# Scaling k by powers of gamma: from one POOL instruction to POOL and ACT, two pairs of heads each

## The chip, the cores and the metric

The program runs on one core of a Trainium2 chip. The metric is the device time of one execution, in microseconds (us). Engines are named as in the profile: PE (matmul; PEld is its weight load), DVE (vector), ACT (scalar), POOL (GpSimd) and SP (which here issues every DMA).

## The reference, cut to what matters

Three layers follow each other, all in float32. The change lies in the first.

```
scores = (q @ k^T) / 8                        # 8 batches, 8 heads, 576 positions, 64 features
ret    = scores * Dmat                        # Dmat[i, j] = gamma_h ** (i - j) for j <= i, else 0
x      = (ret @ v), heads side by side        # 4608 tokens x 512
logits = x @ phi ; d = softmax over tokens ; c = softmax over slots
slot_out = relu((d^T x) @ w1[e]) @ w2[e]      # 8 experts, 4 slots each
y      = c @ slot_out
out    = (((y @ m1) * (y @ m2)) @ w3) @ wo
```

## The kernel before, in words

The attention is done chunk by chunk. A chunk is 64 positions, there are 9 of them, and 8 batches are taken two at a time, so there are 36 steps (`u` from 0 to 35). A step holds two batches and all eight heads, the heads as four pairs. Within a chunk the scores are computed directly. What earlier chunks contribute comes through a running state of 64x64 per head, the sum of k times v. In that sum k of chunk c is multiplied by gamma to the minus position (divided by 8), and the state is multiplied by gamma to the chunk's first position when it is read out. `scale_k(w)` (line 139) does the first of these in place on the k half of the tile `vk`: 128 partitions x 512 elements, which are 2 batches x 4 pairs of heads x 64 features. It multiplies by a table `ktab_sb` that holds one number for each partition, chunk and pair. The first two of its 37 calls, before the loop, go to DVE and the other 35 go to POOL.

The order on each engine is the order in which the program issues, and each engine's queue is worked off in that order. Nothing is moved by a planner. One turn of the loop at line 551 issues, in this order:

- `scale_k(u+2)` on POOL; it waits for the DMA of `vk`, issued three turns earlier by `load_vk`.
- The split of weights. The kernel also turns the float64 weights of the last layer into float32 pieces during the attention. One piece is handled in a turn: an `Abs` on ACT (line 359), then five instructions on DVE (lines 360 to 363 and 354), then an addition on POOL (line 380). For some pieces a copy on ACT (line 385) and a subtraction on POOL (line 390) come a turn later. `run(subs)`, `run_copies()` and `run(adds)` issue these last three, `next_conv` starts the next piece with its `Abs`.
- `emit_qk_pv`: the scores of chunk u+2 (line 159) and the product with v of chunk u (line 161) on PE.
- `emit_p(u+2)`: the scores times the table of powers, DVE, line 167.
- `emit_xt(u)`: the result times its powers, DVE, line 197.
- `emit_state(u+1)`: on PE the new state (line 179, which reads the scaled k of chunks u+1 and u) and the readout of the old one (line 184). Then four instructions on ACT (line 191), one for each pair, that scale the state into SBUF.
- `load_vk(u+5)` and `load_qk(u+6)` on SP, when the buffers are free (six and five of them).
- transposes of x on PE (line 212) with a copy on ACT (line 213), and every fourth turn the logits, the softmax and the slot sums.
- the remaining instructions of the piece of weights on DVE (lines 360 to 354).

So POOL's queue holds in each turn `scale_k`, at times a subtraction, and an addition that waits for DVE's line 354. The `scale_k` of the next turn runs directly behind that addition. ACT's queue holds the copy of the turn before, then the copy or `Abs` for the weights, then the four of line 191.

After the loop the experts run (33.5 MB of weights through the buffers that the attention frees), then the last layer, whose matmuls are at lines 852 to 855.

Of the kernel before, what the change touches and what calls it, by code (L numbers as in the profile page):

```python
# [14 lines left out]
ACTF = mybir.ActivationFunctionType  # L15
ALU = mybir.AluOpType
# [6 lines left out]
NCH = S // 64  # L23
# [7 lines left out]
def retention_softmoe_bilinear(  # L31
# [15 lines left out]
    nc = tc.nc  # L47
# [49 lines left out]
    ktab_sb = tabs_sb[:, 256:292].rearrange("p (c k) -> p c k", c=9)  # L97
# [17 lines left out]
    def four(t):  # L115
        return t.rearrange("p (x k i) -> p x k i", x=2, k=4)

    def qk_tiles(u):
        t = qkb[u % QBUF]
        return four(t[:, 0:512]), four(t[:, 512:1024])  # L120

    def vk_tiles(w):
        t = vkb[(w + 1) % NBUF]
        return four(t[:, 0:512]), four(t[:, 512:1024])
# [6 lines left out]
    def span(w):  # L131
        return slice(0 if w >= 0 else 64, 128 if w < NU - 1 else 64)
# [6 lines left out]
    def scale_k(w, eng=nc.gpsimd):  # L139
        s = span(w)  # L140
        K = vk_tiles(w)[1][s]
        eng.tensor_tensor(  # L142
            out=K, in0=K, in1=ktab_sb[s, w % NCH].unsqueeze(1).unsqueeze(3).to_broadcast([s.stop - s.start, 2, 4, 64]), op=ALU.mult,
        )

    def qk_view(u):
        return four(bank[u % 2])
# [5 lines left out]
    def emit_qk_pv(u, w):  # L153
        for x in range(2):
            for p in range(4):
                for h, a, b in halves:
                    if u is not None:
                        Q, K = qk_tiles(u)
                        nc.tensor.matmul(out=qk_view(u)[a, x, p], lhsT=K[a, x, p], rhs=Q[a, x, p], start=True, stop=True)  # L159
                    if w is not None:  # L160
# [11 lines left out]
    def emit_state(u):  # L172
        c = u % NCH
        for p in range(4):
            for x in range(2):
                for h, a, b in halves:
                    if c < NCH - 1:
                        V, K = vk_tiles(u - h)
                        nc.tensor.matmul(  # L179
                            out=sbank[a, x, p], lhsT=K[a, x, p], rhs=V[a, x, p],  # L180
                            start=(c == 0 and x == 0 and p == 0), stop=True, skip_group_check=True,
# [318 lines left out]
    with tc.manual_schedule():  # L500
# [28 lines left out]
        emit_p(0)  # L529
        load_qk(5)  # L530
        scale_k(-1, nc.vector)
        scale_k(0, nc.vector)
        scale_k(1)
        warm(256)
        emit_qk_pv(1, None)
# [115 lines left out]
        for k in range(4):  # L651
# [7 lines left out]
            out=sme, in0=sT.rearrange("p k (e j) -> p e k j", j=4),  # L659
            in1=rzs.rearrange("p x (e j) -> p e x j", j=4).to_broadcast([128, 8, 4, 4]), op=ALU.mult,  # L660
# [87 lines left out]
        for x in range(2):  # L748
            mw = mw_sb[:, 4096 * x:4096 * x + 4096].rearrange("p (k f) -> p k f", k=4)
            for k in range(4):  # L750
                for g in range(4):
                    nc.tensor.matmul(
                        out=bank[7 - x][32 * g:32 * g + 32, 0:256], lhsT=sot[:, k],
# [56 lines left out]
        for cb in range(8):  # L810
# [7 lines left out]
            if cb == 0:  # L818

                for i, w in enumerate((wh, wl)):  # L820
                    for k in range(8):
                        nc.tensor.matmul(
                            out=bank[6][0:64], lhsT=phl[:, k].rearrange("p x s -> p (x s)"), rhs=w[k],
# [111 lines left out]
```

## Time and profile before

| | |
|---|---|
| median of 3 runs | 458.75 us (458.68, 458.75, 460.63) |
| the profiled execution | 458.34 us, of it span 456.6 us |
| busy in the span: PE / DVE / ACT / POOL | 384.4 / 296.6 / 176.0 / 183.3 us |
| mean granted TensorE clock | 0.933 of full speed |
| the loop over 36 chunks | to about 200 us; the experts to about 303 us; the last layer to the end |

The span goes from the first to the last instruction of the core; the 1.7 us beside it are start and end of the execution. Busy times add over stages with different limits, so the stage has to be looked at by itself.

### The profile page before, as it was taken

The page shows a single profiled execution, that of the slowest core. Times are in us where ns is not written, and L with a number is a line of the kernel's source. Part 1 is how long each engine was busy: PE and PEld are TensorE (multiplying, and loading weights), DVE is VectorE, ACT ScalarE, POOL GpSimd, SP SyncE. Part 2 cuts the span into 40 slices and gives each one's busy share as a digit, 9 for nine tenths or more (in the row PEclk, how much of TensorE's full clock was granted, in tenths as well). Part 3 has the DMA queues.
Part 4 walks back from the last instruction along what each step waited for, and adds up shares of the span by engine and source line. Part 5 has one row for each costly group of instructions (what it writes and reads, how often), then busy time and mean ns, then how long its engine had stood idle before and what let it go on. Part 6 is the DMA issues. An engine that isn't in the chain of part 4 may idle for free.

```text
span 456.6 us, 14422 instructions
## 1 busy us (share of the span) xinstructions
PE 384.4 (84%) x6204; PEld 291.7 (64%) x6204; DVE 296.6 (65%) x497; ACT 176.0 (39%) x410; POOL 183.3 (40%) x148
## 2 busy tenths in 40 slices
PE   6657685968769775979999999977879999999996
PEld 4556564666557654766555665644658888888884
DVE  2224999999989799954698893218996433334420
ACT  0224455543526345522333432122425444444431
POOL 0331566654445445631355453002564444444420
PEclk9887999789888879789999999999989999999999
DMA  8989999899988898774399999959206577888622
GB/s 239 380 309 328 303 334 310 266 305 354 346 291 297 276 359 259 244 246 167 125 341 413 408 410 408 407 181 208 50 10 170 148 222 213 217 210 222 182 76 91
DMA packets 40687, 117.84 MB, mean 258 GB/s; under 512 B 5776, under 2 KB 6288, under 8 KB 40624
## 3 DMA queue, kind: packets, MB, share of 16 engines
q1 hardware_dynamic: 40624, 116.93, 77.1%
q8 instruction: 48, 0.79, 0.7%
q14 instruction: 15, 0.12, 0.1%
HBM read 106.29 MB, written 10.62 MB: 256 GB/s over the span
## 4 chain that ended last, share of the span: by engine, by line
PE 61%; DVE 23%; issue 9%; DMA 4%; ACT 1%; SPq 1%; POOL 0%; DVEq 0%; ACTq 0%
PE bank L852 7%; PE bank L853 7%; PE bank L854 7%; PE bank L421 7%; PE bank L159 5%; PE bank L212 4%; PE bank L179 4%; PE bank L184 3%; DMA vk<-in_v 3%; PE bank L448 3%; PE bank L467 2%; PE bank L161 2%; DVE mw_sb L788 2%; DVE msb L354 2%; PE bank L304 2%
## 5 line engine op out<-in xcount | busy, mean ns | idle before, releaser
L492 POOL TENSOR_TENSOR cc<-mw_sb,cc 128x512 fp32r<-128x512 f32 x36 | 47.8, 1337 | 59.5 <-ACT cc L491 59.5
L191 ACT ACTIVATE st<-bank,msb 128x128 f32<-128x128 f32 x128 | 36.6, 368 | 72.1 <-PE bank L184 59.9
L159 PE MATMUL bank<-qk 64*64 64x64 f32 x1152 | 52.2, 247 | 13.0 <-issue 10.4
L179 PE MATMUL bank<-vk 64*64 64x64 f32 x1024 | 49.2, 245 | 16.2 <-issue 15.8
L184 PE MATMUL bank<-qk,st 64*64 64x64 f32 x1024 | 47.8, 246 | 16.9 <-issue 10.7
L159 PEld LDWEIGHTS bank<-qk 64*64 64x64 f32 x1152 | 46.0, 159 | 21.4 <-issue 16.6
L380 POOL TENSOR_TENSOR vals<-vals,msb 128x512 f32<-128x512 f32 x24 | 31.0, 1292 | 70.6 <-DVE msb L354 60.1
L184 PEld LDWEIGHTS bank<-qk,st 64*64 64x64 f32 x1024 | 42.2, 158 | 22.8 <-issue 15.2
L161 PE MATMUL bank<-pm,vk 64*64 64x64 f32 x1152 | 51.9, 246 | 4.3 <-issue 4.3
L490 DVE TENSOR_TENSOR mw_sb<-raw 128x512 f32<-128x512 f32 x32 | 30.0, 958 | 34.9 <-POOL cc L492 32.9
L179 PEld LDWEIGHTS bank<-vk 64*64 64x64 f32 x1024 | 43.5, 158 | 14.3 <-issue 13.9
L142 POOL TENSOR_TENSOR vk<-vk,msb 128x512 f32<-128x512 f32 (+1 forms) x35 | 39.9, 1140 | 25.1 <-DMA vk<-in_v 25.1
L421 PE MATMUL bank<-wop,w3p 128*128 128x512 f32 x192 | 49.4, 403 | 0.0
L161 PEld LDWEIGHTS bank<-pm,vk 64*64 64x64 f32 x1152 | 45.6, 157 | 4.3 <-issue 4.3
L857 ACT ACTIVATE mw_sb<-bank,rz 128x512 f32<-128x512 f32 x36 | 24.8, 689 | 53.1 <-PE bank L855 30.5
L421 PEld LDWEIGHTS bank<-wop,w3p 128*128 128x128 f32 x192 | 34.9, 190 | 13.6 <-issue 7.1
L167 DVE TENSOR_TENSOR pm<-bank,msb 128x512 f32<-128x512 f32 x36 | 24.7, 686 | 27.8 <-PE bank L159 20.2
L852 PE MATMUL bank<-w3p,cc 128*128 128x512 f32 x108 | 42.4, 392 | 0.0
L853 PE MATMUL bank<-w3p,cc 128*128 128x512 f32 x108 | 42.2, 391 | 0.0
L854 PE MATMUL bank<-w3p,cc 128*128 128x512 f32 x108 | 42.2, 390 | 0.0
L380 POOL TENSOR_TENSOR mw_sb<-mw_sb,msb 128x512 f32<-128x512 f32 x16 | 20.4, 1275 | 41.9 <-DVE msb L354 39.6
L799 PE MATMUL bank<-w,wop 128*128 128x512 f32 x96 | 25.4, 416 | 7.9 <-DVE wop L793 5.2
(143 smaller groups left out, 788.9 us busy)
## 6 DMA issues: line engine op xcount, KB each, us to landing
qk<-in_q SPq DMA_DIRECT2D x36, 512.0 KB, 5.7
vk<-in_v SPq DMA_DIRECT2D x35, 512.0 KB, 6.0
vk<-in_ew SPq DMA_DIRECT2D x33, 512.0 KB, 10.1
qk<-in_ew SPq DMA_DIRECT2D x29, 512.0 KB, 9.7
raw<-expt SPq DMA_DIRECT2D x36, 256.0 KB, 4.5
out_x<-mw_sb SPq DMA_DIRECT2D x36, 256.0 KB, 3.0
raw<-in_m SPq DMA_DIRECT2D x16, 512.0 KB, 5.8
raw<-in_w SPq DMA_DIRECT2D x16, 512.0 KB, 6.4
```

Source lines behind the costliest of these rows:

```text
L142: eng.tensor_tensor(out=K, in0=K, in1=ktab_sb[s, w % NCH].unsqueeze(1).unsqueeze(3).to_broadcast([s.stop - s.start, 2, 4, 64]), op=ALU.mult,)
L159: nc.tensor.matmul(out=qk_view(u)[a, x, p], lhsT=K[a, x, p], rhs=Q[a, x, p], start=True, stop=True)
L161: nc.tensor.matmul(out=xt_view(w)[b, p, 64 * x:64 * x + 64], lhsT=vk_tiles(w - h)[0][a, x, p], rhs=four(pb[w % 4])[a, x, p], start=(w % NC ...
L179: nc.tensor.matmul(out=sbank[a, x, p], lhsT=K[a, x, p], rhs=V[a, x, p], start=(c == 0 and x == 0 and p == 0), stop=True, skip_group_check= ...
L184: nc.tensor.matmul(out=xt_view(u)[b, p, 64 * x:64 * x + 64], lhsT=four(sb[u % 2])[a, x, p], rhs=qk_tiles(u)[0][a, x, p], start=(x == 0 and ...
L191: nc.scalar.activation(out=Sn[:, :, p], in_=sbank[:, :, p], func=ACTF.Copy, scale=stab_sb[:, c + 1, p:p + 1])
L380: nc.gpsimd.tensor_tensor(out=t, in0=t, in1=parts[j % 2], op=ALU.add)
L421: nc.tensor.matmul(out=ps, lhsT=x, rhs=y, start=(k8 == 0 and part == 0), stop=(k8 == 7 and part == 2))
L492: nc.gpsimd.tensor_tensor(out=cl[m], in0=e, in1=ch[m], op=ALU.subtract)
L852: nc.tensor.matmul(out=ob, lhsT=ch[m][:, sl], rhs=gh[m], start=(m == 0), stop=False)
L853: nc.tensor.matmul(out=ob, lhsT=ch[m][:, sl], rhs=gl[m], start=False, stop=False)
L854: nc.tensor.matmul(out=ob, lhsT=cl[m][:, sl], rhs=gh[m], start=False, stop=False)
```

## The change

`scale_k` gives POOL only the first two pairs of heads, that is 128x256 elements in place of 128x512. The other two pairs are scaled by two `activation(Copy)` instructions on ACT, 128x128 elements each, whose scale is the table's column for that pair. They stand directly behind POOL's instruction in the issue order, so at the head of a turn on ACT. The two calls on DVE before the loop keep all four pairs.

```diff
     def scale_k(w, eng=nc.gpsimd):
         s = span(w)
         K = vk_tiles(w)[1][s]
+        t = ktab_sb[s, w % NCH]
+        np = 4 if eng is nc.vector else 2
         eng.tensor_tensor(
-            out=K, in0=K, in1=ktab_sb[s, w % NCH].unsqueeze(1).unsqueeze(3).to_broadcast([s.stop - s.start, 2, 4, 64]), op=ALU.mult,
+            out=K[:, :, 0:np], in0=K[:, :, 0:np],
+            in1=t[:, 0:np].unsqueeze(1).unsqueeze(3).to_broadcast([s.stop - s.start, 2, np, 64]), op=ALU.mult,
         )
+        for p in range(np, 4):
+            nc.scalar.activation(out=K[:, :, p], in_=K[:, :, p], func=ACTF.Copy, scale=t[:, p:p + 1])
```

## Rows read from the trace of the kernel before

**Rows 1.** The page's chain of waits, shares by engine and by line.

```profile
PE 61%; DVE 23%; issue 9%; DMA 4%; ACT 1%; SPq 1%; POOL 0%; DVEq 0%; ACTq 0%
```

**Rows 2.** Busy time by stretch; clock, DMA share and GB/s come last.

```profile
46.00:200.00 154.00, 114.54 (x3817) 92.89 (x3819) 142.15 (x235) 71.57 (x201) 81.05 (x66) 0.86 0.88 302
200.00:296.00 96.00, 94.22 (x773) 59.75 (x771) 63.14 (x140) 30.91 (x69) 33.42 (x25) 0.99 0.86 329
```

**Rows 3.** The chain of waits in order of time: start, us, what.

```profile
68.97 1.39 DVE vals L361
...
102.38 1.15 DVE mw_sb L361
...
111.85 0.27 PE bank L184
...
154.39 0.30 DVE mt L228
...
162.79 0.61 DVE xts L197
```

**Rows 4.** Timeline of DVE in one turn: start, us, line, operation.

```profile
101.83 0.52 DVE L360 TENSOR_SCALAR mw_sb<-mw_sb 128x512 f32<-128x512 f32 x1
102.38 1.14 DVE L361 TENSOR_SCALAR mw_sb<-mw_sb 128x512 uint32<-128x512 uint32 x1
...
107.47 0.68 DVE L360 TENSOR_SCALAR mw_sb<-mw_sb 128x512 f32<-128x512 f32 x1
```

**Rows 5.** Timeline of POOL in the same turn and the next.

```profile
100.79 1.27 POOL L380 TENSOR_TENSOR mw_sb<-mw_sb,msb 128x512 f32<-128x512 f32 x1 [2.35 <-DVE msb L354]
102.02 1.22 POOL L142 TENSOR_TENSOR vk<-vk,msb 128x512 f32<-128x512 f32 x1
...
106.82 1.05 POOL L142 TENSOR_TENSOR vk<-vk,msb 128x512 f32<-128x512 f32 x1
```

**Rows 6.** Timeline of DVE while POOL stood idle.

```profile
36.48 0.43 DVE L361 TENSOR_SCALAR vals<-vals 128x512 uint32<-128x512 uint32 x1
```

**Rows 7.** POOL's groups by line and shape: count, busy, mean ns, idle before.

```profile
L142 POOL TENSOR_TENSOR vk<-vk,msb 128x512 f32<-128x512 f32 x34 | 38.9, 1143 | 25.1 <-DMA vk<-in_v 25.1
L807 POOL TENSOR_TENSOR gs<-mw_sb,gs 128x256 fp32r<-128x256 f32 x1 | 0.9, 937 | 2.6 <-ACT gs L806 2.6
L804 POOL TENSOR_TENSOR mw_sb<-mw_sb,msb 128x256 f32<-128x256 f32 x1 | 0.7, 730 | 27.0 <-ACT msb L759 27.0
```

**Rows 8.** ACT's groups by line and shape.

```profile
L191 ACT ACTIVATE st<-bank,msb 128x128 f32<-128x128 f32 x128 | 36.6, 368 | 72.1 <-PE bank L184 59.9 <-PE bank L179 12.1
L264 ACT ACTIVATE et<-et 128x128 f32<-128x128 f32 x9 | 2.8, 310 | 19.2 <-DVE et L263 19.2
```

**Rows 9.** Timeline of ACT in one turn.

```profile
99.24 1.14 ACT L191 ACTIVATE st<-bank,msb 128x128 f32<-128x128 f32 x4 [3.97 <-PE bank L184]
```

**Rows 10.** DVE's group of line 360 for pieces of m1 and m2.

```profile
L360 DVE TENSOR_SCALAR mw_sb<-mw_sb 128x512 f32<-128x512 f32 x16 | 8.9, 556 | 0.0
```

**Rows 11.** PE's waits from 40 to 200 us: total, times, longest.

```profile
PE bank L159 <- issue: 10.4, 5, 4.8
...
PE bank L184 <- DVE xts L197: 6.2, 6, 1.7
...
PE bank L212 <- issue: 0.3, 1, 0.3
```

**Rows 12.** The page's busy line and its DMA queue for instructions.

```profile
PE 384.4 (84%) x6204; PEld 291.7 (64%) x6204; DVE 296.6 (65%) x497; ACT 176.0 (39%) x410; POOL 183.3 (40%) x148
...
q8 instruction: 48, 0.79, 0.7%
```

**Rows 13.** The issues of line 137 to their landing.

```profile
DMA to landing us min/median/max: 3.3/6.0/8.5
```

**Rows 14.** Timeline of SP and of ACT: a load and its turn's start.

```profile
97.22 1.10 SPq L137 DMA_DIRECT2D vk<-in_v  x1
...
107.92 0.60 ACT L213 COPY xg<-bank 128x512 f32<-128x512 f32 x1
```

## The prediction, made before the change was run

> **What bounds the kernel now.** I read the chain of waits by engine first. PE carries 61% of it, DVE 23%, POOL and ACT together 1% [rows 1]: neither engine that the change touches is on the path by itself. So the question is whom they hold up. Next come the busy times by stretch. All 35 instructions that change run before 200 us, and between 46 and 200 us DVE is busy for 142.15 of 154 us, PE for 114.54, at a clock of 0.86, ACT for 71.57 and POOL for 81.05 [rows 2]. The chain in order of time then shows who leads where: from 68.97 to 111.85 us it runs on DVE without a break, from there on PE to 154.39, on DVE again to about 163.4, and on PE after that [rows 3]. DVE is therefore the path in some 43 + 9 = 52 us; in the rest of the loop PE is.
>
> DVE's timeline shows why it is slow there. Line 361 takes 1.14 us at 102.38 [rows 4], while POOL's scaling runs from 102.02 to 103.24 [rows 5]; the same instruction takes 0.43 us when POOL is idle [rows 6]. It ends 0.28 us after POOL does (103.52 against 103.24). DVE's instruction stands still until POOL's is over. The scaling itself runs directly behind the addition of line 380 (ends 102.06), and its 1.22 us are 0.17 more than the 1.05 it takes a turn later [rows 5]; line 360 holds DVE until 102.35 [rows 4], so POOL lost about that much to it.
>
> **The change, part by part.**
>
> *POOL's half.* The trace has no 128x256 scaling. If the elements set the time, the 1.05 us become some 0.55, and with the 0.17 lost to line 360 some 0.73 in place of 1.22. Line 804, the one plain instruction of that size, took 0.730; line 807, whose output is of another type, 0.937 [rows 7]. I take 0.73, the row nearest in kind: POOL is done 0.49 us earlier. Ends: 1.22 - 0.94 = 0.28 and 1.22 / 2 = 0.61 us.
>
> *What DVE gets.* Line 361 would end at 103.24 - 0.49 + 0.28 = 103.03 in place of 103.52, later than 102.38 + 0.43 = 102.81, so POOL still sets it and the whole 0.49 us comes off. In the turns that also hold a subtraction on POOL, that one starts and ends 0.49 us earlier and frees the DVE instruction behind it as much sooner. In every fourth turn DVE has two short instructions more and only line 360 meets the scaling: 0.68 us at 107.47 [rows 4]. It would run without a wait, some 0.43 as line 361 does, so 0.25 comes off. On DVE's stretches of the chain lie nine scalings: six of the first kind and two of the second before 111.85 us, one of the first between 154 and 163. Sum 7 x 0.49 + 2 x 0.25 = 3.9 us. With the two ends it is 7 x 0.28 + 2 x 0.1 = 2.2 and 7 x 0.61 + 2 x 0.25 = 4.8.
>
> *What of it PE takes up.* PE was waiting for DVE (line 184 on line 197) for 6.2 us in all between 40 and 200 us; that is the most that a faster DVE can give it. It also stood still with no releaser, "issue", in six rows from 10.4 down to 0.3 us, together 33.0 of 160 us [rows 11]. The queue for instructions moved 48 packets [rows 12], and 6204 matmuls and as many weight loads make 258 for each packet: I read the stops as PE waiting for its next block of instructions, behind data at a DMA share of 0.88 [rows 2]. PE comes to such a block whether it was early or late, so I let it lose of the freed time the share that it loses now, 33.0 / 160 = 21%: 3.9 x 0.21 = 0.8 us. Ends: nothing, and all of it.
>
> The Trainium skill ("Runtime: NRT & Kernel Launch", Instruction fetch mechanics) also has PE's instructions fetched in blocks of 256, and calls the cost of crossing a block mostly hidden. The trace disagrees on the second half, with 33.0 us of issue [rows 11]. By the page the 0.8 us would not be lost and the sum would be 3.9.
>
> *ACT's two instructions.* Nearest rows: line 191, which also has the scale in a column of a table and strided halves but reads PSUM, 0.368 us each and four in 1.14 [rows 8, 9], hence a pair in 0.37 + (1.14 - 0.37) / 3 = 0.63; line 264, SBUF to SBUF, 0.310 each [rows 8], a pair at most 0.62. I take 0.63 us, so 35 x 0.63 = 22 us more of ACT's time. It lies in the 72.1 us in which ACT waits for PE before line 191 [rows 8]: the pair stands ahead of that wait. Its cost on the path is put at 0. If the cover is missing, the four of line 191 come up to 0.63 us late, and so does the `Abs` in front of DVE's line 360; for the pieces in the middle of the loop, line 360 never waited (0.0) [rows 10].
>
> *New waits.* ACT now waits for the DMA of k, and its `Abs`, line 191 and line 213 are queued behind. The load of one chunk was issued from 97.22 to 98.32, and ACT came to the head of the turn that scales it at 108.52 [rows 14], 10.2 us after; this is the shortest of the 29 such leads from 40 us on, and the longest landing is 8.5 us [rows 13]. Cost 0. In the first seven turns the transfers set the pace, and POOL waited 25.1 us for them [rows 7]; there the split gives nothing. PE's line 179 has a second producer to wait for, which runs a turn ahead of it: 0.
>
> *Sum.* 3.9 - 0.8 = 3.1 us off the loop. Behind it PE is busy for 94.22 of 96 us to 296 us [rows 2], and the experts' buffers come free that much sooner, so the gain passes on. The profiled execution took 458.34 us, span 456.6 and 1.74 beside it; it becomes 455.2. It lies 0.41 us under the median of the three runs, so I put the median at 455.7, 0.7% less.
>
> **Rivals.**
>
> 1. *PE takes all of it.* From 111.85 to 154.39 us PE is on the chain [rows 3] although DVE is busy for 142.15 of 154 us in the loop [rows 2], so the two are nearly level; and DMA was busy for 0.88 of the loop [rows 2]. A quicker DVE asks for loads sooner, and the blocks of instructions queue behind these. If the 33.0 us of issue grow by what DVE gives, the time stays: 458.0 to 459. Against it: the 6.2 us of waits on DVE are waits that end with line 197 and with nothing else.
>
> 2. *PE gives more than the chain shows.* If every wait of PE on DVE goes, 6.2 us go, and 452.5 is left. The clock could help: it was 0.86 in the loop, where PE stops often, against 0.99 behind it [rows 2]. Against it: scalings outside the nine give DVE time that PE had no use for.
>
> 3. *Slower: ACT waits for POOL's half.* Both instructions write interleaved columns of one tile. If the order between them is kept for the tile as a whole, ACT's pair starts only when POOL's is done, and POOL's runs behind DVE's last instruction on a piece of weights. The place is the head of a turn on ACT: `Abs`, line 191 and line 213 then follow POOL's clock in place of PE's. In the turn shown, ACT was through with line 191 at 100.38 [rows 9]; POOL's half would be done at 102.02 + 0.73 = 102.75 [rows 5], so ACT could stand for some 2 us. It decides from the point where PE is ready for line 191 before ACT is; if that costs 0.5 us in half of some 28 turns, 7 us are lost against 3.1 gained: 458.75 + 3.9 = 462.6. For it: nothing in the trace shows which way such columns are ordered. Against it: the state that line 191 writes is used a turn later.
>
> **How the numbers follow.** Forecast 0.45, rival 1 0.27, rival 2 0.16, rival 3 0.12. About 0.5% (2.3 us) is what a measurement can tell from no change, so faster means under 456.5. The forecast's own range, from the ends above, is 454 to 457.3; some 0.85 of it is faster. Faster 0.38 + 0.16 = 0.54, same 0.07 + 0.25 = 0.32, slower 0.12 and 0.02 from rival 1's far end. Range 452.2 to 459.8: it takes in most of rivals 1 and 2 and leaves out most of rival 3.
>
> **What would show it.** POOL's instruction near 0.73 us and ACT's near 0.37; line 361 at 0.9 us or less where it took 1.14; DVE's turn in the middle of the loop 0.5 us shorter; PE's wait on line 197 well under 6.2 us; PE's issue not much over 33 us; the logits after the loop some 3 us earlier. Wrong: a DVE stretch as long as before though its instructions are shorter (rival 1, if issue has grown), or ACT idle behind POOL at its new line (rival 3).

## The result and the profile after

| | before | changed |
|---|---|---|
| median of 12 executions each | 460.36 us | 457.14 us |
| the profiled execution (its span) | 458.34 us (456.6) | 457.15 us (455.3) |
| busy DVE / ACT / POOL | 296.6 / 176.0 / 183.3 us | 287.4 / 196.3 / 167.9 us |

The ratio is 0.9886, 95% interval 0.985 to 0.9922. Executions of either kernel differ by more than the effect (452.0 to 462.6 us for the changed one), and the ratios leave disturbed executions out while the medians hold them all; so ratios are compared below, and medians only where they are named. Three more measurements of the same changed kernel gave 0.995, 0.9912 and 0.9979. The mean of the four is 0.993, some 3 us less than before. By the medians the four gains are 3.2, 1.0, 2.1 and 0.6 us, so the size is known to a few us only.

The page's chain by engine answers to [rows 1]: DVE's share falls from 23 to 13%, PE's rises, and issue with it.

```profile
PE 67%; DVE 13%; issue 11%; DMA 5%; ACT 1%; SPq 1%; DVEq 0%; ACTq 0%
```

Busy time by stretch, with clock, DMA share and GB/s last, answers to [rows 2]. DVE now leaves 20 of 154 us idle where it left 12, and PE's clock in the loop is 0.89 where it was 0.86.

```profile
46.00:200.00 154.00, 113.89 (x3868) 93.00 (x3862) 134.10 (x236) 87.11 (x258) 69.62 (x67) 0.89 0.87 303
200.00:296.00 96.00, 93.30 (x732) 58.18 (x733) 61.03 (x136) 30.43 (x67) 32.58 (x25) 1.00 0.87 334
```

The chain in order of time, against [rows 3]. DVE holds it from 66.25 to 76.6 us and from 152.61 to 156.8, together 14.6 us in place of 52. The lines have moved: 365 is 360, 366 is 361, 202 is 197, 189 is 184, 385 is 380, 144 is 142.

```profile
66.25 0.30 DVE mt L233
...
75.98 0.61 DVE xts L202
76.63 0.27 PE bank L189
...
145.69 0.59 ACT xg L218
146.28 0.59 ACT vk L149 x2
146.87 0.57 ACT mw_sb L364
147.44 2.59 issue
...
152.61 0.30 DVE mt L233
...
156.20 0.61 DVE xts L202
```

DVE's timeline in mid-loop, as [rows 4]:

```profile
93.31 0.52 DVE L365 TENSOR_SCALAR mw_sb<-mw_sb 128x512 f32<-128x512 f32 x1
93.87 0.72 DVE L366 TENSOR_SCALAR mw_sb<-mw_sb 128x512 uint32<-128x512 uint32 x1
...
98.25 0.72 DVE L366 TENSOR_SCALAR mw_sb<-mw_sb 128x512 uint32<-128x512 uint32 x1
...
102.91 0.41 DVE L365 TENSOR_SCALAR mw_sb<-mw_sb 128x512 f32<-128x512 f32 x1
```

and POOL's, as [rows 5]:

```profile
92.28 1.27 POOL L385 TENSOR_TENSOR mw_sb<-mw_sb,msb 128x512 f32<-128x512 f32 x1 [2.35 <-DVE msb L359]
93.51 0.80 POOL L144 TENSOR_TENSOR vk<-vk,msb 128x256 f32<-128x256 f32 x1
...
102.27 0.61 POOL L144 TENSOR_TENSOR vk<-vk,msb 128x256 f32<-128x256 f32 x1
```

POOL's scaling ends at 94.31 and line 366 at 94.59, again 0.28 us later: it still waits for POOL, only for less. Two turns are 98.25 - 93.87 = 4.38 us apart. Before, the same instruction started at 97.58 and 102.38 [rows 3, 4], 4.80 apart:

```profile
97.58 1.14 DVE L361 TENSOR_SCALAR mw_sb<-mw_sb 128x512 uint32<-128x512 uint32 x1
```

The mean over the 16 of this kind, before and after:

```profile
L361 DVE TENSOR_SCALAR mw_sb<-mw_sb 128x512 uint32<-128x512 uint32 x16 | 14.5, 904 | 0.4
```

```profile
L366 DVE TENSOR_SCALAR mw_sb<-mw_sb 128x512 uint32<-128x512 uint32 x16 | 9.5, 595 | 0.4
```

ACT's two instructions, all but the pair on 64 partitions:

```profile
L149 ACT ACTIVATE vk<-vk,msb 128x128 f32<-128x128 f32 x68 | 24.3, 417 | 3.4 <-DMA vk<-in_v 3.4
```

PE's waits from 40 to 200 us, against [rows 11]: DVE falls from 6.2 to 1.9 us. The six rows of issue add up to 39.9 us where they were 33.0.

```profile
PE bank L189 <- issue: 11.6, 6, 3.1
PE bank L164 <- issue: 8.6, 5, 2.7
PE bank L166 <- issue: 8.5, 6, 2.6
PE bank L184 <- issue: 8.4, 7, 1.8
PE bank L189 <- DVE xts L202: 1.9, 2, 1.0
PE bank L217 <- issue: 1.6, 1, 1.6
PE bank L227 <- issue: 1.2, 1, 1.2
```

In this one execution PE's first matmul of line 426, which follows the loop, starts at 204.6 us; line 421's started at 207.3 before. The windows up to there, before and after, hold the same matmuls. PE was busy for 5.7 us less, at a granted clock of 0.89 for 0.86, and stood still for 3.0 us more (58.4 for 55.4).

```profile
0.00:207.30 207.30, 151.92 (x4857) 124.08 (x4857) 160.25 (x267) 85.95 (x246) 92.96 (x81) 0.86 0.89 302
```

```profile
0.00:204.60 204.60, 146.22 (x4856) 118.94 (x4857) 150.78 (x266) 106.13 (x315) 77.52 (x81) 0.89 0.88 307
```

In the profiles of the three later measurements that matmul starts at 209.2, 206.0 and 207.2: one execution does not show a gain of this size, the ratios do. Of the 2.65 us of the first profile 1.3 are left in the span. The rest is lost near 300 us: line 472's sixteen matmuls took 1.85 us for one expert and 3.33 for the last. PE had stood idle for some 2 us ahead of them, as it had before the change. The windows of that stretch, of before and of after, have the granted clock third from the end: 1.00 (2.4 GHz throughout) and 0.79 (part of it at 1.2 GHz).

```profile
290.21 1.85 PE bank L472 x16
...
298.52 3.33 PE bank L472 x16
```

```profile
296.00:304.00 8.00, 5.37 (x62) 2.88 (x61) 1.47 (x3) 1.81 (x4) 0.00 (x0) 1.00 0.72 245
```

```profile
296.00:304.00 8.00, 5.01 (x33) 1.73 (x32) 1.76 (x4) 1.23 (x3) 0.00 (x0) 0.79 0.53 148
```

### The profile page after: what moved, and what is told of

Its sections match the earlier page's. It is cut to its first block, busy times and chain, and to the rows that moved or that the text cites. A ratio compares the mean times of both kernels' runs of the same rounds, so it can differ in the third digit from the quotient of the medians.

```text
span 455.3 us, 14500 instructions
## 1 busy us (share of the span) xinstructions
PE 380.3 (84%) x6204; PEld 287.1 (63%) x6204; DVE 287.4 (63%) x497; ACT 196.3 (43%) x480; POOL 167.9 (37%) x148
## 4 chain that ended last, share of the span: by engine, by line
PE 67%; DVE 13%; issue 11%; DMA 5%; ACT 1%; SPq 1%; DVEq 0%; ACTq 0%
PE bank L857 7%; PE bank L858 7%; PE bank L859 7%; PE bank L426 6%; PE bank L164 6%; PE bank L217 5%; PE bank L189 4%; PE bank L184 4%; PE bank L166 3%; PE bank L227 3%; PE bank L453 3%; PE bank L472 2%; PE bank L309 2%; DMA vk<-in_ew 2%; PE bank L804 2%
## 5 line engine op out<-in xcount | busy, mean ns | idle before, releaser
L184 PE MATMUL bank<-vk 64*64 64x64 f32 x1024 | 46.9, 241 | 17.2 <-issue 17.1
L196 ACT ACTIVATE st<-bank,msb 128x128 f32<-128x128 f32 x128 | 36.5, 367 | 55.3 <-PE bank L189 38.3
L164 PE MATMUL bank<-qk 64*64 64x64 f32 x1152 | 49.9, 238 | 12.4 <-issue 8.6
L189 PE MATMUL bank<-qk,st 64*64 64x64 f32 x1024 | 47.3, 242 | 15.1 <-issue 13.0
L166 PE MATMUL bank<-pm,vk 64*64 64x64 f32 x1152 | 50.2, 238 | 8.5 <-issue 8.5
L164 PEld LDWEIGHTS bank<-qk 64*64 64x64 f32 x1152 | 43.4, 150 | 19.9 <-issue 13.5
L189 PEld LDWEIGHTS bank<-qk,st 64*64 64x64 f32 x1024 | 41.8, 155 | 19.5 <-issue 17.0
L184 PEld LDWEIGHTS bank<-vk 64*64 64x64 f32 x1024 | 41.4, 154 | 15.9 <-issue 15.9
L166 PEld LDWEIGHTS bank<-pm,vk 64*64 64x64 f32 x1152 | 43.7, 150 | 10.0 <-issue 10.0
L426 PEld LDWEIGHTS bank<-wop,w3p 128*128 128x128 f32 x192 | 34.9, 190 | 13.6 <-issue 7.1
L144 POOL TENSOR_TENSOR vk<-vk,msb 128x256 f32<-128x256 f32 (+1 forms) x35 | 24.6, 702 | 26.6 <-DMA vk<-in_v 26.6
```

Of the source, the lines that this page charges most:

```text
L166: nc.tensor.matmul(out=xt_view(w)[b, p, 64 * x:64 * x + 64], lhsT=vk_tiles(w - h)[0][a, x, p], rhs=four(pb[w % 4])[a, x, p], start=(w % NC ...
L184: nc.tensor.matmul(out=sbank[a, x, p], lhsT=K[a, x, p], rhs=V[a, x, p], start=(c == 0 and x == 0 and p == 0), stop=True, skip_group_check= ...
L189: nc.tensor.matmul(out=xt_view(u)[b, p, 64 * x:64 * x + 64], lhsT=four(sb[u % 2])[a, x, p], rhs=qk_tiles(u)[0][a, x, p], start=(x == 0 and ...
L196: nc.scalar.activation(out=Sn[:, :, p], in_=sbank[:, :, p], func=ACTF.Copy, scale=stab_sb[:, c + 1, p:p + 1])
L426: nc.tensor.matmul(out=ps, lhsT=x, rhs=y, start=(k8 == 0 and part == 0), stop=(k8 == 7 and part == 2))
```

## The experiments

Ratios are to the kernel before on the same chip, with 95% intervals, over five rounds each.

**The changed kernel three times more** (no edit).

> The changed kernel, once more beside the others on the same chip. Theory (a shorter POOL instruction holds DVE up for less time): 0.985 to 0.993 of the time before, PE's wait on line 202 near 2 us where it was 6.2, its issue near 40 where it was 33. Rival (chance in where PE meets its blocks of instructions): the ratio moves by more than 0.5% from the first, towards 1.

> The changed kernel a third time: the first two gave 0.9886 and 0.995, and their intervals only just meet. Theory (a gain of 3 to 4 us): 0.988 to 0.995. Rival (the gain is a matter of the chip and the hour): outside that.

> The changed kernel beside it. Both theories: 0.987 to 0.996; what counts is the distance to POOL's half alone.

0.995 (0.991 to 0.999), 0.9912 (0.987 to 0.9955) and 0.9979 (0.994 to 1.0018). The first and the last miss their range by 0.002, and the first lies over 0.5% nearer to 1 than 0.9886, as its rival said. The interval of the last holds 1. PE's wait on DVE was 1.0, 2.6 and 1.4 us, its issue 45.1, 38.3 and 42.1. With all four ratios below 1 the gain is taken as real, but it is smaller than the first measurement said.

**The gain without ACT's part.**

```diff
-        for p in range(np, 4):
-            nc.scalar.activation(out=K[:, :, p], in_=K[:, :, p], func=ACTF.Copy, scale=t[:, p:p + 1])
```

> POOL scales two pairs of heads, nobody scales the other two (that part of the scaling is left out). Theory: DVE is held up exactly as little as with the change and ACT's pair of instructions lies in its waits for PE, so the time is that of the changed kernel within 0.3%. Rival (ACT's 29 us of added work cost something on the path, in front of line 196 or of the Abs): faster than the changed kernel by 0.5% or more. Rival (chance): any place between 0.985 and 1.0.

> POOL's half alone a second time, beside the changed kernel: the first time it stood at 0.9864 and the changed kernel at 0.995 on the same chip, so whether ACT's pair of instructions costs anything is open. Theory (it lies in ACT's waits): within 0.4% of the changed kernel. Rival (it costs): again 0.6% or more faster than the changed kernel.

0.9864 (0.9813 to 0.9916) and 0.9929 (0.9893 to 0.9965). Beside the changed kernel on the same chip that is 0.9 and 0.5% less, by the medians 0.4 and 0.6% (457.43 for 459.28 us, 457.75 for 460.43). The first is what the rival expected; the second lies between theory and rival. The theory that ACT's pair costs nothing does not hold up well: both differences go the same way, though the intervals overlap. Neither the cost nor its size is shown; 0.7% would be 3 us.

**ACT's part without the gain.** POOL scales all four pairs.

```diff
+        np = 4
...
+        if eng is not nc.vector:
+            V = vk_tiles(w)[0][s]
+            for p in (2, 3):
+                nc.scalar.activation(out=scr[s], in_=V[:, :, p], func=ACTF.Copy, scale=t[:, p:p + 1])
```

> POOL scales all four pairs as before, and ACT carries the two added instructions all the same: they scale two pairs of v into a small spare tile that nobody reads (they write bfloat16, because no more space is free). So ACT's load is that of the change and POOL's hold on DVE that of before. Theory: no gain, ratio 0.997 to 1.004; line 361's counterpart on DVE back at 1.14 us in mid-loop, PE's wait on DVE back at 5 to 7 us. Rival (the gain has to do with ACT's clocking or with the order on ACT, not with POOL's length): 0.985 to 0.993 here too.

0.9995 (0.9952 to 1.0037). The gain is gone. The waits of PE in this kernel, largest first, say why (line 192 reads the state out, line 205 is DVE's 197, line 369 its 361):

```profile
PE bank L192 <- DVE xts L205: 13.6, 12, 2.0
PE bank L167 <- issue: 7.4, 5, 4.6
```

```profile
L369 DVE TENSOR_SCALAR mw_sb<-mw_sb 128x512 uint32<-128x512 uint32 x16 | 14.5, 905 | 0.4
```

DVE's instruction is back at 0.905 us in the mean of 16 (0.595 with the change), and PE waits for DVE longer than it did before, 13.6 us where 5 to 7 were expected, with 27.2 of issue in 19 stops. So the gain comes from POOL's length, not from anything on ACT. The same load on ACT costs nothing measurable here, where PE waits for DVE the more.

**POOL in two halves.**

```diff
-        eng.tensor_tensor(out=K, ...)
+        for o, n in ((0, 4),) if eng is nc.vector else ((0, 2), (2, 2)):
+            eng.tensor_tensor(out=K[:, :, o:o + n], ...)
```

> POOL scales all four pairs, but in two instructions of 128x256 each; ACT does nothing. Theory (DVE stands still until the POOL instruction that runs is over): line 361's counterpart gets in between the two, so it shortens in mid-loop from 0.90 to some 0.6 us in the mean, and the next one (line 362's counterpart, which was never held in mid-loop, 0.693) is held by the second half and lengthens to 0.9 or more; DVE's turn is no shorter, time 0.995 to 1.006. Rival (what counts is only how early the first two pairs are done): 0.985 to 0.993, as the change.

0.9942 (0.9886 to 0.9998), a little under what I expected. The median, 462.07 us, is not below that of the kernel before on this chip, 460.23, so no gain is shown. DVE's groups in mid-loop (364 is 361, 365 is 362), and line 362 before:

```profile
L365 DVE SCALAR_TENSOR_TENSOR mw_sb<-raw,mw_sb 128x512 uint32<-128x512 uint32 x16 | 14.3, 896 | 0.5
...
L364 DVE TENSOR_SCALAR mw_sb<-mw_sb 128x512 uint32<-128x512 uint32 x16 | 10.7, 669 | 0.4
```

```profile
L362 DVE SCALAR_TENSOR_TENSOR mw_sb<-raw,mw_sb 128x512 uint32<-128x512 uint32 x16 | 11.1, 693 | 0.5
```

The first gets 0.904 - 0.669 = 0.235 us shorter, the next 0.896 - 0.693 = 0.203 longer. DVE gets in between two POOL instructions and stands still for the one that runs, so the wait moves to the next instruction and hardly shrinks. The Trainium skill ("SBUF — State Buffer", SBUF: two separate sides) says of the shared port pair that GpSimd and certain VectorE instructions take it as an exclusive lock, for a whole instruction. These rows agree, and so does the 0.28 us after POOL's end in the turns shown, before and after.

**All four pairs on ACT.** `np` is 0 on POOL, so POOL does none.

> ACT scales all four pairs, POOL none. Theory: DVE is no longer held by the scaling at all: line 366 at 0.43 to 0.45 us in mid-loop; but PE waited only 1.9 us on DVE any more, so of DVE's further 0.25 us a turn at most 1 to 2 us reach the end: 0.981 to 0.990 of the time before. Rival (ACT becomes the bound or delays line 196 and the Abs: 35 x 1.4 = 49 us more than before the change): slower than the changed kernel by 0.5% or more.

> All four pairs on ACT once more, on the same chip as the changed kernel. Theory (PE's issue bounds the loop, so nothing more is to be had from DVE): within 0.4% of the changed kernel on either side. Rival (DVE's further 0.3 us a turn still reaches the end): faster than the changed kernel by over 0.5%.

0.9885 (0.9822 to 0.9948) and 0.9924 (0.9878 to 0.997); the changed kernel stood at 0.995 beside the first and at 0.9912 beside the second. DVE's instruction is at 0.424 us in the mean of the second, as free as with POOL idle. The two comparisons with the changed kernel point opposite ways, and the intervals overlap, so nothing more reaches the end that could be told from the change. In the second measurement PE's issue was 38.2 us, and it waited 1.8 us for DVE. A better version is not shown.

```profile
L367 DVE TENSOR_SCALAR mw_sb<-mw_sb 128x512 uint32<-128x512 uint32 x16 | 6.8, 424 | 0.4
```

**Fewer bytes in the loop.**

```diff
+        n = 512 if j < 5 else 64
-        nc.sync.dma_start(out=raws[j % 5].bitcast(I64), in_=pieces[j])
+        nc.sync.dma_start(out=raws[j % 5].bitcast(I64)[:, 0:n], in_=pieces[j][:, 0:n])
```

> The kernel before, with the pieces of weights from the sixth on loaded to one eighth (64 of 512 columns; the rest of the tile keeps older data, so the split weights are not the right ones). It takes some 0.45 of 1.57 MB a turn off the DMA engines and leaves every instruction in place. Theory of the instruction blocks (PE's issue is its next block of instructions waiting behind data): PE's issue between 40 and 200 us falls from 33 to under 20 us, its wait on DVE rises over 10 us since DVE's turn of 4.8 us is now the slower one, and the time falls by 5 us or more: 0.975 to 0.99. Rival (the stops have nothing to do with the data): issue stays at 28 to 38 us, time 0.993 to 1.0.

> The changed kernel with the same light loads. If the blocks of instructions wait behind data, DVE bounds the loop here, and the 0.49 us a turn of the split come through in most of some 30 turns: 6 to 13 us under the kernel before with light loads, so 0.95 to 0.975 of the time before. Rival (PE's stops are as many as ever): 3 to 5 us under it, as with full loads.

> All four pairs on ACT with the light loads (weights from the sixth piece on loaded to one eighth). With light loads PE still waited 12.5 us for DVE under the split; DVE's line 361 counterpart goes from 0.72 to 0.43 us. Theory: some 3 to 7 us under the split with light loads, 0.951 to 0.960 of the time before. Rival (ACT's two further instructions cost as much as DVE gains, in front of the state's scaling): 0.963 to 0.972.

0.9869 (0.982 to 0.9919) for the kernel before, 0.9666 (0.9612 to 0.972) with the split, 0.956 (0.9511 to 0.9609) with all four pairs on ACT. All three lie in the ranges of their theories. The same split is now worth 2.1% (medians of 454.78 against 445.3 us), and the step to four pairs, from which nothing could be told with full loads, another 1.1% (measured on another chip). PE's waits in the kernel before with light loads, and then with the split:

```profile
PE bank L184 <- DVE xts L197: 21.3, 16, 2.3
PE bank L184 <- issue: 8.2, 5, 2.6
PE bank L159 <- issue: 2.7, 1, 2.7
PE bank L179 <- issue: 2.5, 3, 1.1
PE bank L161 <- issue: 1.6, 1, 1.6
PE bank L212 <- issue: 1.1, 1, 1.1
```

```profile
PE bank L189 <- DVE xts L202: 12.5, 10, 2.7
PE bank L189 <- issue: 8.7, 5, 3.2
PE bank L164 <- issue: 3.7, 2, 2.6
PE bank L184 <- issue: 3.3, 4, 1.3
PE bank L227 <- issue: 3.1, 1, 3.1
PE bank L166 <- issue: 2.6, 2, 1.6
PE bank L217 <- issue: 1.0, 1, 1.0
```

Issue falls to 16.1 from 33.0 and to 22.4 from 39.9, although not one instruction of PE was changed. The stops get fewer and hardly shorter: 11 for 21 before the change and 15 for 26 with it, 1.5 us each for 1.6 and 1.5. PE also waits for DVE longer, by 15.1 and 10.6 us, and POOL whole with the pair on ACT shows less issue beside a longer wait with the loads left full (27.2 beside 13.6 us). So part of the fall may be stops that pass unseen while PE waits for DVE; what the bytes do to the stops by themselves was not separated. What the times show is that with fewer bytes more of what DVE gains reaches the end.

## Why the prediction was right

The direction, the place and about the size were right, and the mechanism that was named first, POOL's hold on DVE, was shown. The agreement in size (0.7% forecast, 0.7% in the mean of the four ratios) is in part luck: the term of POOL and DVE was nearly met, but those of PE and ACT were not.

- *POOL's half.* 0.80 us in mid-loop where 0.73 was put, 0.61 where nothing is in its way (0.55). POOL is done 0.42 us earlier and not 0.49, and DVE's turn is shorter by just that. Where line 365 alone met the scaling, 0.68 became 0.41, as put.
- *What DVE gets.* With 0.42 the sum is 7 x 0.42 + 2 x 0.25 = 3.4 us for 3.9. That the gain hangs on POOL's length was shown by putting the length back (0.9995).
- *What PE takes up.* The mechanism was named, its size was not right: PE's wait on DVE fell by 4.3 us, but issue rose by 6.9 in the first profile (and by 12.1, 5.3 and 9.1 in the three others), where I had 0.8. "PE's issue not much over 33 us" was among the signs, and it failed. PE did not lose that much in the end, since POOL's half alone gave 0.9864 and 0.9929, some 4.8 us (3.1 by the medians), no less than the 3.1 put down. PE's times do not show where the gain arises. The time in which it stood still grew (waits on DVE and issue together from 39.2 to 41.8, 46.1, 40.9 and 43.5 us). What fell is its busy time up to line 426, which the sum left as it was: from 151.9 to 146.2, 147.4, 148.0 and 147.7 us, at a granted clock of 0.86 and then 0.89, 0.87, 0.88 and 0.87. But with POOL whole and the pair on ACT it was 147.7 too, at 0.89, without a gain. So it is not shown that the clock carries the gain, nor that the change raised it.
- *The stops.* That the stops of issue are the blocks of instructions themselves rests on the count of 258 instructions for a packet [rows 12] and on time: all 14 stops of 0.9 us or more before, and 20 of 21 with the change, have a packet of that queue that starts between 1.6 us before and 2.2 us after the stop begins, with packets some 5 us apart. The fetch was not taken away by itself. That the stops cap the gain is argued: the same split is worth 9.5 us with light loads, but there more than the stops differs.
- *ACT's two instructions, put at 0.* They take 0.417 us each in the mean, a pair in mid-loop 0.69 to 0.74, where 0.63 was put. An estimate from the figures of the Trainium skill ("ScalarE: Activation LUTs", What ACT_TABLE_LOAD costs, on ACTIVATE's time) is 386 ns for one such instruction and 679 for a pair; the shortest single one here was 386. The pair is not always hidden: at 146.28 us it stands on the chain between line 218 and the `Abs`, 0.59 us. The two comparisons with POOL's half alone put the cost at 2 to 4 us, the run with POOL whole and the pair on ACT at nothing; so the 0 is in doubt and not refuted. Where a cost would arise was not found: between 40 and 200 us PE's waits on ACT in the four profiles of the changed kernel come to 0.9 us at most, and DVE waited for ACT in none.
- *New waits.* ACT waited 3.4 us for the DMA of k, three times, all in the first turns; later never. Right.
- *Rivals.* The second, the larger gain, fits the first measurement (0.9886) better than the forecast did, and the mean of four does not. The third was wrong: no row has ACT waiting for POOL at line 149. The first rival's condition came true, issue grew by more than the wait on DVE fell, but the time did not stay, by the mean of the four.

## What to carry to other kernels

An engine that is nowhere on the chain can still set the pace: look for one instruction on the busy engine with two durations, and for whose end the long one shares. Shorten the instruction that holds the other engine up, rather than cut it in two; and before counting on the whole gain, look at how near the next engine is and what it stops for: here the same split was worth some three times as much with a lighter DMA load. When the gain is below 1%, measure it several times, since the ratios of one kernel ran from 0.9886 to 0.9979. That a queue is idle on average does not make work moved into it free: price it by a run that leaves it out.

## What the runs showed of the hardware

PE's stops without a releaser took 27 to 45 us of the 160 with full loads: 33.0 before, 27.2 where PE waited 13.6 us for DVE, 38.3 to 45.1 where it waited 1.0 to 2.6. With the weights' loads cut to an eighth (DMA share 0.69 for 0.88) they fell to 16.1 beside 21.3 us of waiting for DVE, fewer and not shorter. DVE's line 361, where it meets POOL's scaling, ended 0.28 us after it, before the change and with it; with the scaling in two POOL instructions, DVE got an instruction in between them. And a clock step can undo a gain in one execution: 1.48 us more for the last expert's sixteen matmuls, in a stretch with a granted clock of 0.79.
